# An attention and mixture-of-experts kernel: the order of work after the last attention pair, and the place of a fill

## The chip, the cores and the metric

The kernel runs on one core of a Trainium2 chip. That core has five engines that run their own instruction streams and meet at semaphores: TensorE (PE in the profile), VectorE (DVE), ScalarE (ACT), GpSimd (POOL) and SyncE (SP), which here only issues transfers. The metric is device time in microseconds, the median of several executions. Profiles are of one execution each.

## The reference

Two stages. First a chunked attention: for 4 batches, 8 heads, 768 positions and head size 64, each chunk of 32 queries sees 8 memory keys, 16 positions to its left, itself and 8 to its right. Its output, 3072 tokens of 512 values, goes into a mixture of experts with one always-active dense branch:

```python
h_dense = np.maximum(x @ w1_dense, 0.0)
y_dense = h_dense @ w2_dense
logits = x @ w_gate                      # 512 x 8
expert_idx = np.argmax(logits, axis=1)
gate_w = probs[np.arange(N), expert_idx] # softmax of the logits
for e in range(E):
    mask = expert_idx == e
    h = np.maximum(x[mask] @ w1[e], 0.0)
    y_moe[mask] = gate_w[mask, None] * (h @ w2[e])
return y_dense + y_moe
```

Each token goes to one of eight experts, so which rows an expert multiplies is known only once its gate has been computed.

## The kernel before

**Order.** The engines' orders are written by hand: the kernel opens a manual schedule (line 121), so each engine executes its instructions in the order in which the Python code emits them. A wait in one engine's order holds all that stands behind it on that engine, and nothing on the others.

**Attention.** A loop over 16 pairs of heads (i = 0 to 15; four pairs to each batch, b is the batch) is staged over pairs: while pair i has its probabilities turned and multiplied with the values (probs_back, values, scaled), pair i + 1 has its queries and keys turned and its scores and softmax computed, and pair i - 1 goes through gate_part (its output is transposed into xT32 in fp32 for the gate and into xTb in bf16 for the dense layers) and gate_sum (its share of the logits). What follows from a complete batch is worked off in the next batch's pairs: choose (largest logit, one-hot, differences), weight_exp and weight (the gate's weight), rank (each token's row in the expert order, row_i), and for each of six tiles of 128 tokens dense_1 and dense_2 (the dense branch) and row_out.

**The records in DRAM.** row_out scatters a tile's records with an indirect transfer issued by POOL into x_rec, a DRAM tensor with a region of rows for each expert. A record of 3080 bytes holds the token in bf16, its gate weight, its number and its dense result. So what an expert needs is found in consecutive rows. One transfer of 3080 KB, the fill (lines 779 to 784), writes some finite record into the 128 rows ahead of each expert's region, since a last, short tile of an expert can reach back into them.

**The experts.** 31 slots of 128 records. The first R1 = 11 (round one) are full tiles that surely can be made of the first three batches' records; lists_1a and lists_1b compute which rows and which expert each has. The other 20 (round two) need all four batches; lists_2a, 2b and 2c compute theirs. For a slot s: fetch(s) loads 128 records into a tile xg (394 KB, SP's queue, eleven buffers); transposed(s) turns the tokens on TensorE into at_ps and ACT copies them to xT; staged(s) copies the expert's first weights to w_st on DVE; first_layer(s) is 16 matmuls and a ReLU on ACT; second_layer(s) is 4 matmuls, then DVE forms y (times gate weight, plus the dense result), POOL computes the destinations and issues the scatter of y to the output. The first fetch waits until every record written so far has landed (lines 649 to 656), as does the first fetch of round two.

**After the last pair** (lines 852 to 904): the eleven fetches of round one, gate_part(15), then the transposes of slots 0 and 1, gate_sum(15), the first layer of slot 0, choose, and so on: batch 3's gate, dense tiles and row_outs are interleaved with round one's slots, one dense tile to one slot, transposes one slot ahead. Round two transposes two slots ahead.

**Shared places.** The transposes of slots, the gate's sums, the choice's turned logits, ranks and counts lie in one PSUM tile, at_ps; dense_1, dense_2 and gate_part rotate through two PSUM buffers (tag tp); w_st has three buffers, y five.

Of the kernel before, what the change touches and what calls it, by code (L numbers as in the profile page):

```python
# [20 lines left out]
def kernel(  # L21
# [14 lines left out]
    nc = tc.nc  # L36
# [12 lines left out]
    T = S // 128  # L49
# [10 lines left out]
    E = moe_w_gate.shape[1]  # L60
# [32 lines left out]
    R1 = -(-((N_tokens - S) - E * 127) // 128)  # L93
# [14 lines left out]
    REC = YD + D_moe  # L108
# [3 lines left out]
    x_rec = nc.dram_tensor("x_rec", [N_rows, REC], F32, kind="Internal").ap()  # L112
    rows_written = []

    def scattered(ins, group):

        tc.declare_no_dep(ins.ins, group=group, reason="rows of tokens are distinct")
        tc.add_to_no_dep_group(group, ins.ins)
# [5 lines left out]
    with (  # L124
# [35 lines left out]
        NPAIR = B * NP  # L160
# [175 lines left out]
        def gate_part(pi):  # L336

            b, hp = divmod(pi, NP)
            xb = st_[pi].pop("x")
            if hp == 0:  # L340
                lg_b = x_pool.tile([GP, GT], F32, tag="lg")
                rec_b = x_pool.tile([128, T, REC], F32, tag="rec")
                xTb_b = x_pool.tile([128, NP, S], BF16, tag="xTb")
                bat[b].update(lg=lg_b, rec=rec_b, xTb=xTb_b, h={})
            rec, xTb = bat[b]["rec"], bat[b]["xTb"]
            nc.gpsimd.tensor_copy(  # L346
                rec.bitcast(BF16)[:, :, hp * 128:(hp + 1) * 128], xb
            )
            last = pi == NPAIR - 1
            xT32 = g_work.tile([128, S], F32, tag="xT32")  # L350
            st_[pi]["xT"] = xT32
            for t0 in (0, T // 2):
                xtt = a_ps2.tile([128, 512], F32, tag="tp")
                cols = slice(t0 * 128, (t0 + T // 2) * 128)
                for t in range(T // 2):
                    nc.tensor.transpose(  # L356
                        xtt[:, t * 128:(t + 1) * 128], xb[:, t0 + t, :], identity_f32
                    )
                nc.scalar.copy(xT32[:, cols], xtt[:, :T // 2 * 128])  # L359

                if last:
                    nc.vector.tensor_copy(xTb[:, hp, cols], xtt[:, :T // 2 * 128])
            if not last:
                nc.gpsimd.tensor_copy(xTb[:, hp, :], xT32)  # L364
# [280 lines left out]
        def fetch(s):  # L645
            row = entry(SP_, 0, s, r_sp, N_rows - 128)
            xg = m_load.tile([128, REC], F32, tag="xg")
            ins = nc.sync.dma_start(xg, x_rec[bass.ds(row, 128), :])
            while rows_written:
                tc.add_manual_dep(  # L650
                    ins.ins, rows_written.pop(),
                    mybir.DependencyInfo(
                        mybir.DependencyClass.Sync, mybir.DependencyReason.DATA
                    ),
                    reason="the rows in DRAM",
                )
            xgs[s] = xg
            if s < R1:
                first_round.append(ins.ins.name)

        def transposed(s):
            xtp = at_b[:, 2 * (s % 2):2 * (s % 2) + 2, :].rearrange(
                "p a (d t) -> p (a d) t", t=128
            )
            xgb = xgs[s].bitcast(BF16)
            for d in range(DT):
                nc.tensor.transpose(  # L667
                    xtp[:, d, :], xgb[:, d * 128:(d + 1) * 128], identity
                )
            xT = m_work.tile([128, DT, 128], BF16, tag="xT")  # L670
            nc.scalar.copy(xT, xtp)  # L671
            xTs[s] = xT

        def staged(s):

            e = entry(DVE_, 1, s, e_dve, E - 1)
            w_st = w_work.tile([128, DT, F], BF16, tag="w_st")
            nc.vector.tensor_copy(w_st[:, None], w1_all[:, bass.ds(e, 1), :, :])  # L678
            w_sts[s] = w_st

        def first_layer(s):
            xT, w = xTs.pop(s), w_sts.pop(s)
            ph = sc[:, s % 2, :].rearrange("p (f t) -> p f t", t=128)
            for f in range(FT):
                for d in range(DT):
                    nc.tensor.matmul(  # L686
                        ph[:, f, :], w[:, d, f * 128:(f + 1) * 128], xT[:, d, :],
                        start=(d == 0), stop=(d == DT - 1),
                    )
            h_sb = m_work.tile([128, FT, 128], BF16, tag="h")  # L690
            nc.scalar.activation(h_sb, ph, AF.Relu)  # L691
            hs[s] = h_sb
# [75 lines left out]
        for i in range(NPAIR):  # L768
            nxt = i + 1 < NPAIR
            b, hp = divmod(i, NP)  # L770

            mine = [2 * hp - 2, 2 * hp - 1] if b and hp else []
            if b == B - 1:
                mine = [[], [0, 1], [2, 3, 4], [5]][hp]
            for t in bat[b - 1].pop("ready", []) if b else []:
                row_out(b - 1, t)
            if i == NPAIR - 2:

                ins = nc.sync.dma_start(
                    x_rec.rearrange("(e r) c -> r e c", e=E)[:128],  # L780
                    bat[b - 1]["rec"][:, 0:1, :].to_broadcast([128, E, REC]),
                )
                scattered(ins, "rows")
                rows_written.append(ins.ins.name)
            if i + 2 < NPAIR:
                load_qk(i + 2)
                load_v(i + 2)
            if nxt:
                transpose_qk(i + 1)
            if i == NPAIR - 1:  # L790
                lists_1b()
            probs_back(i)
            if hp == 1 and b:
                choose(b - 1)
            for t in mine[:1]:
                dense_1(b - 1, t)
            if i:
                gate_part(i - 1)
            if nxt:
                scores(i + 1)  # L800
                next_rows(i + 1, 1)
                if hp == 1 and b:
                    weight_exp(b - 1)
                softmax(i + 1)
                next_rows(i + 1, 0)
                if hp == 1 and b:
                    weight(b - 1)
            for t in mine[:1]:
                dense_2(b - 1, t, nc.vector.tensor_copy if nxt else nc.scalar.copy)
            later = list(mine)  # L810
            if mine and hp > 1:
                row_out(b - 1, later.pop(0))
            for t in mine[1:]:
                dense_1(b - 1, t)
                if t != mine[-1]:
                    dense_2(b - 1, t, nc.scalar.copy)
                    row_out(b - 1, later.pop(0))
            if i:
                gate_sum(i - 1)
            if i == NPAIR - 1:  # L820
                for s in range(2):
                    staged(s)
            values(i)
            scaled(i)
            for t in mine[1:]:
                if t == mine[-1]:
                    dense_2(b - 1, t, nc.scalar.copy)
            bat[b - 1]["ready"] = later
            for _ in range(1 if i + 3 < NPAIR else 2):
                if w_todo:  # L830
                    load_w(*w_todo.pop(0))
            if hp == 1 and b:
                rank(b - 1)
            if hp == NP - 1 and b:
                for t in bat[b - 1].pop("ready"):
                    row_out(b - 1, t)
            if i == NPAIR - 2:
                lists_1a()
# [12 lines left out]
        b = B - 1  # L851
        for s in range(R1):
            fetch(s)
        gate_part(NPAIR - 1)
        transposed(0)
        transposed(1)
        gate_sum(NPAIR - 1)
        first_layer(0)
        choose(b)
        dense_1(b, 0)  # L860
        first_layer(1)
        weight_exp(b)
        rank(b)
        weight(b)
        dense_2(b, 0, nc.scalar.copy)
        row_out(b, 0)
        second_layer(0)
        transposed(2)
        staged(2)
        lists_2a()  # L870
        for s in range(2, R1):
            t = s - 1
            if t < T:
                dense_1(b, t)
            first_layer(s)
            if t < T:
                dense_2(b, t, nc.scalar.copy)
                row_out(b, t)
            if s + 1 < R1:
                transposed(s + 1)  # L880
                staged(s + 1)
            second_layer(s - 1)
            if s == 2:
                lists_2b()
            if s == 3:
                lists_2c()
        second_layer(R1 - 1)
        for s in range(R1, R1 + 4):
# [47 lines left out]
```

## Time and profile before

| what | us |
|---|---|
| median of 3 runs | 291.83 (290.97 to 292.04) |
| the profiled execution | 290.2 |
| its span, first to last instruction | 288.5 |
| TensorE busy | 214.0 (74%) |
| VectorE, ScalarE, GpSimd busy | 157.8, 134.8, 135.2 |
| mean granted TensorE clock | 0.905 of full |

The span is the time between the first and the last instruction of one execution; the execution's time lies 1.7 us above it. TensorE is the busiest engine, but a share of busy time is an average over stages. The chain of work that ended last is put together at 46% from TensorE, 16% from transfers, 14% from stretches in which nothing visible was waited for, and 10% from VectorE. The attention pairs end near 186 us, round one of the experts runs from 195 to 237, round two from there to 282. The lines of the profile that bear on the change are shown where the prediction uses them. In a timeline line the numbers are start and duration in us, then the engine, the code line, the operation, output and input; in brackets how long the engine had been idle and what ended that.

### The profile page before, as it was taken

What the parts mean: (1) busy time and instruction counts of PE and PEld (TensorE: products, weight loads), DVE (VectorE), ACT (ScalarE), POOL (GpSimd) and SP (SyncE); (2) the same over time, 40 slices, a digit from 0 to 9 for tenths busy, and PEclk for the clock granted to TensorE, in tenths of its full rate; (3) what the DMA queues carried; (4) which work ended last, traced back from release to release, by engine and by line L of the source; (5) the groups of instructions that cost most, each with busy time, mean ns of one, the idle gap of its engine ahead of it and who ended that gap; (6) DMA issues with size and microseconds to landing.
All of it is one profiled execution on the core that took longest, in us unless ns stands there. A gap on an engine that the chain in (4) does not pass through costs nothing.

```text
span 288.5 us, 10781 instructions
## 1 busy us (share of the span) xinstructions
PE 214.0 (74%) x4559; PEld 160.4 (56%) x4559; DVE 157.8 (55%) x320; ACT 134.8 (47%) x204; POOL 135.2 (47%) x209
## 2 busy tenths in 40 slices
PE   1576838669987739888658878517999868999980
PEld 1455637465755537656437656316677546777740
DVE  2675465746556445675363853832774445766640
ACT  2362646526755516556153673312456435455430
POOL 7054244512674922375470455510357742665661
PEclk9999598769999968999795999965999999999997
DMA  6999998995999996999999799959534599896220
GB/s 106 191 149 166 170 161 136 178 179 76 199 174 195 193 219 94 188 183 165 184 209 185 100 305 370 204 176 366 224 121 184 195 350 412 278 303 233 101 73 0
DMA packets 59440, 55.51 MB, mean 192 GB/s; under 512 B 35966, under 2 KB 51326, under 8 KB 59392
## 3 DMA queue, kind: packets, MB, share of 16 engines
q0 software_dynamic: 20560, 31.49, 52.9%
q1 hardware_dynamic: 38832, 23.33, 34.6%
q8 instruction: 36, 0.59, 0.9%
q14 instruction: 12, 0.10, 0.1%
HBM read 51.62 MB, written 20.74 MB: 251 GB/s over the span
## 4 chain that ended last, share of the span: by engine, by line
PE 46%; DMA 16%; issue 14%; DVE 10%; ACT 5%; POOL 4%; SPq 2%; POOLq 1%; DVEq 0%; ACTq 0%
PE sc L686 9%; PE av L699 7%; PE ph L461 7%; PE pd L475 4%; PE at_ps L300 4%; DMA t__2065<-in_k_dram 3%; PE xtt L356 3%; DVE mx L285 3%; DMA t__3050<-in_k_dram 3%; PE tp_f L242 3%; DMA x_rec<-rec_b,row_i 3%; PE sc L276 2%; PE at_ps L667 2%; DMA t__2550<-in_k_dram 2%; DVE vw L199 2%
## 5 line engine op out<-in xcount | busy, mean ns | idle before, releaser
L486 POOL DMA_INDIRECT x_rec<-rec_b,row_i x24 | 24.7, 1029 | 58.0 <-issue 21.7
L715 POOL DMA_INDIRECT out_dram<-y,dst x31 | 31.7, 1021 | 25.5 <-DVE w_st L678 12.2
L712 DVE SCALAR_TENSOR_TENSOR y<-av,xg 128x512 f32<-128x512 f32 x31 | 23.3, 751 | 29.2 <-PE av L699 23.7
L285 DVE TENSOR_REDUCE mx<-sc 128x12 f32<-128x768 f32 x16 | 15.3, 958 | 39.3 <-PE sc L276 39.3
L686 PEld LDWEIGHTS <-w_st 128*128 128x128 bf16 x496 | 30.9, 100 | 8.8 <-issue 3.2
L686 PE MATMUL sc<-xT,w_st 128*128 128x128 bf16 x496 | 33.9, 223 | 1.8 <-DVE w_st L678 0.6
L699 PE MATMUL av<-w_all,h_sb 128*128 x124 | 31.8, 379 | 2.7 <-DVE y L712 1.7
L691 ACT ACTIVATE h_sb<-sc 128x512 bf16<-128x512 f32 x31 | 18.5, 597 | 31.4 <-PE sc L686 28.6
L364 POOL CAST xTb_b<-xT 128x768 bf16<-128x768 f32 x15 | 12.4, 829 | 36.4 <-ACT xT L359 36.3
L461 PE MATMUL ph<-xTb_b,w1d 128*128 128x128 bf16 x384 | 28.8, 235 | 0.0
L461 PEld LDWEIGHTS <-w1d 128*128 128x128 bf16 x384 | 26.5, 107 | 3.9 <-issue 0.8
L475 PE MATMUL pd<-w2d,h_d 128*128 128x512 bf16 x96 | 24.9, 381 | 5.0 <-DVE rec_b L479 5.0
L199 ACT COPY vw<-vw 24x1536 f32<-24x1536 f32 x16 | 23.5, 1468 | 10.6 <-DMA vw<-in_v_dram 10.3
L312 PE MATMUL av<-vw,at 64*32 64x65 f32 x1536 | 22.1, 237 | 8.2 <-issue 7.6
L312 PEld LDWEIGHTS av<-vw,at 64*32 64x32 f32 x1536 | 18.2, 110 | 16.7 <-issue 14.4
L254 DVE COPY dT<-tp_f 128x768 bf16<-128x768 bf16 x16 | 15.3, 955 | 20.3 <-PE tp_f L242 19.9
L356 PE MATMUL xtt<-identity_f,x_p 128*128 128x128 f32 x96 | 19.4, 333 | 8.3 <-DVE x_p L324 3.2
L300 PE MATMUL at_ps<-identity_f,a_sb 128*128 128x128 f32 x96 | 19.2, 355 | 7.2 <-issue 4.3
L671 ACT COPY xT<-at_ps 128x512 bf16<-128x512 bf16 x31 | 18.1, 584 | 9.1 <-PE at_ps L667 9.0
L346 POOL CAST rec_b<-x_p 128x768 bf16<-128x768 f32 x16 | 13.4, 835 | 19.1 <-DVE x_p L324 16.6
L678 DVE COPY w_st<-w_all 128x2048 bf16 x31 | 21.2, 693 | 1.8 <-DMA w_all<-in_moe_w_dram 0.9
L252 ACT COPY dT<-tp_f 128x768 bf16<-128x768 bf16 x16 | 12.7, 794 | 19.9 <-PE tp_f L242 19.8
(231 smaller groups left out, 366.9 us busy)
## 6 DMA issues: line engine op xcount, KB each, us to landing
xg<-x_rec SPq DMA_DIRECT2D x31, 385.0 KB
w_all<-in_moe_w_dram POOLq DMA_DIRECT2D x16, 512.0 KB
vw<-in_v_dram SPq DMA_DIRECT2D x32, 184.0 KB
x_rec<-rec_b SPq DMA_DIRECT2D x1, 3080.0 KB
vw<-in_mem_v_dram SPq DMA_DIRECT2D x32, 48.0 KB
vw<-in_v_dram SPq DMA_DIRECT2D x64, 4.0 KB
w1d<-in_moe_w_dense_dram POOLq DMA_DIRECT2D x1, 512.0 KB
w2d<-in_moe_w_dense_dram POOLq DMA_DIRECT2D x1, 512.0 KB
```

Source lines behind the costliest of these rows:

```text
L199: copy(vt[p0 + CHUNK:p0 + CTX, :NCH, :D], vt[p0:p0 + CTX - CHUNK, 1:NCH + 1, :D],)
L285: nc.vector.reduce_max(mx, scv, axis=AX.X)
L300: nc.tensor.transpose(at_ps[:, t, :], a_sb[:, t, :], identity_f32)
L312: nc.tensor.matmul(av[cc * CHUNK:(cc + 1) * CHUNK, hh, t * (D + 1):(t + 1) * (D + 1)], at[p0:p0 + KEYS, t, cc * CHUNK:(cc + 1) * CHUNK], v ...
L356: nc.tensor.transpose(xtt[:, t * 128:(t + 1) * 128], xb[:, t0 + t, :], identity_f32)
L461: nc.tensor.matmul(ph[:, f * 128:(f + 1) * 128], w1d_sb[:, d, f * 128:(f + 1) * 128], xTb[:, d, t * 128:(t + 1) * 128], start=(d == 0), st ...
L475: nc.tensor.matmul(pd, h_d[:, f * 128:(f + 1) * 128], w2d_sb[:, f, :], start=(f == 0), stop=(f == FT - 1),)
L486: ins = nc.gpsimd.indirect_dma_start(x_rec, bass.IndirectOffsetOnAxis(ap=row_i[:, n:n + 1], axis=0), bat[b]["rec"][:, t, :], None,)
L686: nc.tensor.matmul(ph[:, f, :], w[:, d, f * 128:(f + 1) * 128], xT[:, d, :], start=(d == 0), stop=(d == DT - 1),)
L699: nc.tensor.matmul(py, h_e[:, f, :], w2_all[:, bass.ds(e, 1), f, :], start=(f == 0), stop=(f == FT - 1),)
L712: nc.vector.scalar_tensor_tensor(y, py, xg[:, GW:GW + 1], xg[:, YD:], op0=ALU.mult, op1=ALU.add)
L715: ins = nc.gpsimd.indirect_dma_start(out, bass.IndirectOffsetOnAxis(ap=dst, axis=0), y, None, bounds_check=N_tokens - 1, oob_is_err=False,)
```

## The change

The fill moves from pair 14 to behind the eleven fetches of round one on the same queue, and is declared independent of all of these but the last, on which it waits. The copies of the first two slots' weights (staged(0), staged(1)) leave pair 15. After the last pair each engine's order begins with batch 3's gate sum, choice, dense tiles, ranks and row_outs; transposes of slots 0 and 1 come before the last dense tile, and then round one's slots follow one another, transposed two ahead.

```diff
-            if i == NPAIR - 2:
-                ins = nc.sync.dma_start(x_rec... [:128], bat[b - 1]["rec"]...)
-                scattered(ins, "rows")
-                rows_written.append(ins.ins.name)
...
             if i:
                 gate_sum(i - 1)
-            if i == NPAIR - 1:
-                for s in range(2):
-                    staged(s)
             values(i)
             scaled(i)
...
         for s in range(R1):
             fetch(s)
+        ins = nc.sync.dma_start(x_rec... [:128], bat[b - 1]["rec"]...)
+        scattered(ins, "rows")
+        rows_written.append(ins.ins.name)
+        for f in first_round[:-1]:
+            tc.declare_no_dep(ins.ins, f, reason="those tiles are full without these")
         gate_part(NPAIR - 1)
-        transposed(0)
-        transposed(1)
         gate_sum(NPAIR - 1)
-        first_layer(0)
+        dense_1(b, 0)
         choose(b)
-        dense_1(b, 0)
-        first_layer(1)
+        for t in range(2):
+            dense_1(b, t + 1)
+            dense_2(b, t, nc.scalar.copy)
         weight_exp(b)
         rank(b)
         weight(b)
-        dense_2(b, 0, nc.scalar.copy)
         row_out(b, 0)
-        second_layer(0)
-        transposed(2)
-        staged(2)
+        row_out(b, 1)
+        dense_1(b, 3)
+        dense_2(b, 2, nc.scalar.copy)
+        row_out(b, 2)
+        for s in range(2):
+            staged(s)
+        dense_1(b, 4)
+        dense_2(b, 3, nc.scalar.copy)
+        row_out(b, 3)
         lists_2a()
-        for s in range(2, R1):
-            t = s - 1
-            if t < T:
-                dense_1(b, t)
+        for s in range(2):
+            transposed(s)
+        dense_1(b, 5)
+        dense_2(b, 4, nc.scalar.copy)
+        row_out(b, 4)
+        for s in range(R1):
             first_layer(s)
-            if t < T:
-                dense_2(b, t, nc.scalar.copy)
-                row_out(b, t)
-            if s + 1 < R1:
-                transposed(s + 1)
-                staged(s + 1)
-            second_layer(s - 1)
-            if s == 2:
+            if s == 0:
+                dense_2(b, 5, nc.scalar.copy)
+                row_out(b, 5)
+            if s + 2 < R1:
+                transposed(s + 2)
+                staged(s + 2)
+            if s:
+                second_layer(s - 1)
+            if s == 0:
                 lists_2b()
-            if s == 3:
+            if s == 1:
                 lists_2c()
         second_layer(R1 - 1)
```

More of the change, by code (lines that the diff above doesn't have):

```diff
@@ L776 @@
                 row_out(b - 1, t)
-            if i == NPAIR - 2:
[L779 to L782, printed above, removed]
-                scattered(ins, "rows")
-                rows_written.append(ins.ins.name)
             if i + 2 < NPAIR:
@@ L853 @@
             fetch(s)
+        ins = nc.sync.dma_start(
+            x_rec.rearrange("(e r) c -> r e c", e=E)[:128],
+            bat[b - 1]["rec"][:, 0:1, :].to_broadcast([128, E, REC]),
+        )
+        scattered(ins, "rows")
+        rows_written.append(ins.ins.name)
+        for f in first_round[:-1]:
+            tc.declare_no_dep(ins.ins, f, reason="those tiles are full without these")
         gate_part(NPAIR - 1)
-        transposed(0)
-        transposed(1)
         gate_sum(NPAIR - 1)
-        first_layer(0)
+        dense_1(b, 0)
         choose(b)
-        dense_1(b, 0)
-        first_layer(1)
+        for t in range(2):
+            dense_1(b, t + 1)
+            dense_2(b, t, nc.scalar.copy)
         weight_exp(b)
```

## The prediction

> **What bounds the kernel now.** I read the chain of work that ended last, then TensorE's timeline around the places it names, then the granted clock by stretches, then what the SyncE (SP) queue waits for. The change touches only work from the last pair (i = 15) on, so I start at 180 us. The chain there:
>
> ```profile
> 184.13 7.27 DMA x_rec<-rec_b,row_i
> ...
> 191.71 3.22 DMA xg<-x_rec
> 194.93 0.05 issue
> 194.98 0.62 PE at_ps L667 x4
> ...
> 198.56 1.82 PE sc L686 x16
> ...
> 200.62 1.71 PE ph L461 x16
> ```
>
> The last scatter of batch 2's rows (row_out, tile 5) takes 7.27 us to land, the first gathered tile another 3.22 us, and only then TensorE does transposed(0), which stands in its order ahead of batch 3's gate sum and all dense work. Those need no gathered row. TensorE's timeline shows the hole, and the stretch in which round one closes:
>
> ```profile
> 185.34 0.34 PE L312 MATMUL av<-vw,at 64*32 64x65 f32 x15 [1.11 <-issue]
> 188.85 1.34 PE L356 MATMUL xtt<-identity_f,x_p 128*128 128x128 f32 x6 [3.17 <-DVE x_p L324]
> 194.98 0.61 PE L667 MATMUL at_ps<-identity,xg 128*128 128x128 bf16 x4 [4.78 <-DMA xg<-x_rec]
> ...
> 228.05 1.05 PE L686 MATMUL sc<-xT,w_st 128*128 128x128 bf16 x16 [0.56 <-ACT xT L671]
> ...
> 236.08 1.02 PE L699 MATMUL av<-w_all,h_sb 128*128 x4 [0.84 <-DVE y L712]
> ...
> 239.05 1.07 PE L686 MATMUL sc<-xT,w_st 128*128 128x128 bf16 x16 [0.61 <-DVE w_st L678]
> ```
>
> From 185.68 to 194.98 TensorE works 1.34 us. Round one's last second layer starts at 236.08 and ends 0.87 later, at 236.95: that is the mark I carry the sum to. What comes after (round two, tail) has the same code before and after: 288.5 - 236.95 = 51.6 us. The granted clock, in stretches cut where it switches (columns: stretch, length, busy us of PE, its weight loads, DVE, ACT, POOL, then clock, DMA share, GB/s):
>
> ```profile
> 49.10:52.52 3.42, 1.47 (x12) 1.26 (x12) 2.61 (x5) 1.69 (x3) 1.19 (x2) 1.00 1.26 176
> 52.52:55.93 3.41, 3.41 (x165) 2.21 (x163) 2.07 (x3) 2.50 (x4) 2.46 (x4) 0.50 1.27 205
> 185.63:189.05 3.42, 0.25 (x10) 0.23 (x3) 2.40 (x4) 0.00 (x0) 0.28 (x1) 1.00 1.10 287
> 189.05:192.46 3.41, 1.15 (x6) 0.75 (x4) 1.11 (x2) 0.96 (x2) 0.68 (x2) 0.50 0.15 61
> 199.29:202.70 3.41, 3.41 (x35) 3.41 (x33) 1.66 (x9) 0.88 (x2) 0.00 (x0) 0.50 1.01 404
> 205.00:230.00 25.00, 23.69 (x275) 17.35 (x274) 14.94 (x38) 13.84 (x26) 16.83 (x25) 1.00 0.42 162
> 245.00:260.00 15.00, 15.00 (x188) 11.59 (x187) 10.33 (x16) 7.86 (x15) 9.48 (x16) 1.00 0.90 292
> ```
>
> After the hole the clock is half until 202.70, so the first expert and dense tiles run at 1.82 and 1.71 us where later ones take 0.89. From 205 TensorE is the bound (23.69 of 25 us), with the transfers at a share of 0.42; from 245 it is busy throughout at 1.98 us a slot, with transfers at 0.90.
>
> **The change, part by part.** *Fill off the front of SP's queue.* One DMA of 3080 KB, issued at 163.57, whose 1024 packets of 3080 B I count at 168.1 to 183.9 us (all but 12 or so by 179.7). It stood among batch 2's scatters and two weight loads of 512 KB, which ran at about 180 GB/s from 182 to 188 with two scatters of tile rows queued behind them on POOL's queue. Without it those weights start when issued, near 178, end near 184, and the last scatter, issued by POOL at 184.13, needs no more than one in an idle stretch: the one issued at 225.58 let the next gather go at 229.16, 3.6 us. So gathers start near 188.4 instead of 191.7. It saves nothing by itself, because after the reorder TensorE asks for xg(0) near 200; its value is that the eleven gathers (191.71 to packets' end at 206.1, 14.4 us) end about 3 us sooner.
>
> *staged(0), (1) off DVE's front.* They hold DVE from 185.27 (0.93 us for the weights, 1.29 us of copies) and push scaled(15): rs at 187.42. Without them rs starts when values end, 185.7, x_p is done at 187.0, and the transposes start at 187.15 instead of 188.85: 1.7 us. The copies now go behind row_out(2), where DVE waits on dense work anyway; first_layer(0) comes near 203, so they are covered by some 4 us.
>
> *New order on TensorE.* From 187.15 to the end of second_layer(10), at full clock: transposes 2 x 0.50 (the three at 180.40); wait for ACT's second copy 0.6 (0.48 plus hand-overs); gate sum 0.65; dense 6 x (0.89 + 0.88) = 10.6; choice, ranks, count 0.5; 11 transposes of 0.23 = 2.5; 11 first layers of 0.89 = 9.8; 11 second layers of 0.87 = 9.6. Waits that stay or come: transposed(0) behind DVE's read of the count, and transposed(1) behind ACT's copy, since all share at_ps (before: 0.67 at 196.26): 1.0 together; second_layer(10) behind y(9), 0.84 as before. Sum 37.1 us.
>
> *Half clock.* Stretches with 1.47 and 1.39 us of work in 3.41 were followed by half clock, one with 1.89 was not. After the change the stretch to 189.05 holds about 1.0 + 0.25, so I expect a drop, and one full stretch (as 52.52:55.93) to end it: 3.41 / 2 = 1.7 us lost. Bounds: 0 if it stays up, 3.4 for a second stretch. The Trainium skill's page "TensorE: Matmul & The Clock Gate" (HAM oscillation) warns only of idle gaps above about 3.4 us; the gap left here is 1.5 us, and by that rule the loss would be nothing and the sum 1.7 us lower. The rows above, busy 43% and followed by a drop, speak against that reading, and I go by them.
>
> So second_layer(10) ends at 187.15 + 37.1 + 1.7 = 226.0, against 236.95: 10.95 us. Cross-check: round one's dense tiles no longer sit between slots, each slot transposes two ahead as round two does, and runs at round two's 1.98 us; before, the slots from 225.35 came every 2.3 to 2.9 us.
>
> *ACT, DVE, POOL.* ACT has 1.2 us per dense pair of 1.78 and 1.18 per slot of 1.98. DVE has y 0.75 + weights 0.69 per slot, plus three list parts of about 2 us, the first before the slots; it catches up by slot 4. POOL's six scatters (0.2 + 0.3 + 1.0) run from about 197.5 to 206, before the first y. Nothing there delays TensorE; cover gone, a list part would cost one slot 1 us.
>
> *Fill behind the gathers.* Here the change adds a wait. SP holds the fill until gather 10 lands, and gathers of round two stand behind it and wait for it to land (fetch(11) takes every row written). Before:
>
> ```profile
> SPq L648 <- DMA x_rec<-rec_b,row_i: 15.3, 2, 12.0
> ```
>
> fetch(11) hung on row_out(5) and went at 229.16, 7.8 us ahead of its use at 236.94. After: gathers to 203, and about 2.3 us more as up to three scatters of 394 KB share the engines: fill issued near 206. Its first packet came 4.5 us after issue before, a gather's 1.0: take 2.5. Then 3.15 MB plus half of the scatters left and 0.13 MB/us of output rows: the mixed rate after 168 was 360 to 400 GB/s, so 12 to 14 us, landing near 222. fetch(11) lands 3.2 us later, 225.5; TensorE wants it at 226.0. That is no slack, so I charge 1.0 us. Lower bound 0. Upper bound: issue to last packet as before, 20.3 us: landing at 227, xg(11) at 230.4, a stall of 4.4. I take 1.0 because the old tail (179.7 to 183.9) lay among the weight loads, which are gone by then. The page "DMA: Bandwidth & Descriptors" of the skill (Latency and other measured facts) speaks against the move: it gives HBM access 0.2 us on average but 2 us under high load, and this wait chains two landings in a saturated stretch; by it I would estimate some 2 us more of stall, and no row here isolates that.
>
> *Output buffers.* y has five. Scatters land late beside the fill, outputs queue behind them; y(5) near 218 needs out(0), issued near 209 and landing near 216. Covered by 2 us; gone, it adds to the same stall.
>
> **Sum.** 10.95 - 1.0 = 9.95 us. The profiled execution took 290.2 us with a span of 288.5, so 280.2; the runs' median, 291.83, stands 1.6 above it, so 281.8, stated as 282.0.
>
> **The rivals.** *R1, round two's loads come late*: fill at its old 20.3 us, or outputs held up beside it; stall 3 to 7 us. For it: no slack at 226, DMA at 1.0 share from 198 to 222. Against: work before it is only 1.2 MB of scatters, and later gathers at 1.3 us each overtake 1.98 us slots. 285 to 289. *R2, the clock stays down or the dense chain stalls*: two further half stretches, or ACT late on a PSUM buffer at each tile (two rotate): 2 to 4 us, 284 to 286. Against: from 199.29 one busy stretch brought it back. *R3, better*: the clock never drops and xg(11) is early: 282.0 - 2.7 = 279.3. *R4, slower*: the fill alone decides. For the time to stay, xg(11) must come at 237, so the fill must land at 233.5, 27 us after issue, 7 beyond its old 20.3; slower by over 0.5% from 29 us on. Since nothing but outputs competes then, that needs a rate below 115 GB/s for the fill: unlikely, at about 293 to 296. *R5, the change does nothing* would need TensorE's hole to be refilled by a wait of batch 3's own gate, which needs only x_p: no row for it.
>
> **How the numbers follow.** Forecast with stall 0 to 3 us: 0.56 (280.5 to 284); R1 0.18, R2 0.09, R3 0.11, R4 and R5 0.06. Low end: R3 at 279. High end: R1 to 288. A measurement of this kernel tells 0.5% (1.5 us) from no change. Faster 0.93; same 0.02 (end of R1, R5); slower 0.05 (R4).
>
> **What would show it.** No TensorE wait on xg near 190; L356 at about 187; dense tiles at 0.89 from about 193; second layer 10 ending near 226; the fill issued near 206 and fetch(11) near 222; TensorE idle at the round boundary 2 to 3 us. Wrong, if after 226 TensorE waits on xg for over 3 us, if half clock goes on beyond 196, or if the second round's slots are longer than 1.98 us.

## The result, and the profile after

| | before | changed |
|---|---|---|
| median, 6 runs each, us | 291.94 (290.97 to 293.17) | 284.93 (280.4 to 289.8) |
| the profiled execution, us | 290.2 | 289.8 |
| its span, us | 288.5 | 288.1 |
| end of the last value products (attention) | 185.69 | 187.68 |
| from there to the end of the last second layer | 95.0 | 92.6 |

The ratio of times is 0.9668, with a 95% interval of 0.9604 to 0.9731: the changed kernel is faster by 3.3%. This ratio, like those below, leaves out executions more than 1.5% above the fastest of their kernel, three of the changed kernel's six among them; the medians of all six give 0.976. The forecast was 282.0 us, in a range of 279 to 288.

The profiled execution is the slowest of the six, and it can't be read without knowing that executions of this kernel differ by some us in the attention stage, long before anything in the change. In the fourteen profiles of this study the value products of pair 12 begin anywhere from 144.4 to 152.6 us. Marks below therefore count from the end of the last value products.

The hole that the forecast started from is gone. TensorE's timeline, changed kernel:

```profile
186.50 1.18 PE L312 MATMUL av<-vw,at 64*32 64x65 f32 x96
189.94 1.50 PE L356 MATMUL xtt<-identity_f,x_p 128*128 128x128 f32 x6 [2.26 <-DVE x_p L324]
...
194.18 1.06 PE L461 MATMUL ph<-xTb_b,w1d 128*128 128x128 bf16 x16
195.07 1.03 PE L475 MATMUL pd<-w2d,h_d 128*128 128x512 bf16 x4
...
201.92 0.38 PE L667 MATMUL at_ps<-identity,xg 128*128 128x128 bf16 x4 [0.28 <-DVE cnt L584]
202.98 0.38 PE L667 MATMUL at_ps<-identity,xg 128*128 128x128 bf16 x4 [0.67 <-ACT xT L671]
...
209.42 1.02 PE L699 MATMUL av<-w_all,h_sb 128*128 x4 [0.81 <-issue]
...
228.27 1.02 PE L699 MATMUL av<-w_all,h_sb 128*128 x4 [1.77 <-issue]
...
232.00 1.02 PE L699 MATMUL av<-w_all,h_sb 128*128 x4 [0.84 <-DVE y L712]
236.37 0.61 PE L667 MATMUL at_ps<-identity,xg 128*128 128x128 bf16 x4 [3.35 <-DMA xg<-x_rec]
```

Dense tiles (L461, L475) fill the place where TensorE waited for the first gathered tile, and transposed(0) starts without a wait on its data. A new wait stands at the boundary of the rounds: second_layer(10) ends near 233.0 and TensorE then waits 3.35 us for the first gather of round two. The granted clock fell to half during this wait, at 234.33, and stayed there until 241.16 us, so the first slots of round two ran slowly as well. The chain of work that ended last names what held it:

```profile
201.95 16.81 DMA xg<-x_rec
...
218.81 13.37 DMA x_rec<-rec_b
...
232.38 3.95 DMA xg<-x_rec
...
236.37 0.62 PE at_ps L667 x4
```

The last gather of round one was issued at 201.95 and took 16.8 us; only then did the fill go out, which took 13.4; only then fetch(11). What SP's queue waited for says the same (L844 is the fill):

```profile
SPq L844 <- DMA xg<-x_rec: 16.5, 1, 16.5
SPq L648 <- DMA x_rec<-rec_b: 12.1, 1, 12.1
```

### The profile page after: what moved, and what is told of

The parts are those of the page before. It is cut to its first block, busy times and chain, and to the rows that moved or that the text cites. A ratio compares the mean times of both kernels' runs of the same rounds, so it can differ in the third digit from the quotient of the medians.

```text
span 288.1 us, 10795 instructions
## 1 busy us (share of the span) xinstructions
PE 215.2 (75%) x4559; PEld 161.1 (56%) x4559; DVE 158.7 (55%) x320; ACT 134.7 (47%) x204; POOL 136.1 (47%) x209
## 4 chain that ended last, share of the span: by engine, by line
PE 34%; DMA 31%; issue 14%; DVE 10%; POOL 4%; ACT 3%; SPq 2%; POOLq 1%; DVEq 0%; ACTq 0%
DMA vw<-in_v_dram 12%; DMA xg<-x_rec 7%; PE ph L461 5%; PE sc L686 5%; DMA x_rec<-rec_b 5%; PE av L699 4%; PE at_ps L300 4%; DMA t__2065<-in_k_dram 3%; PE xtt L356 3%; PE tp_f L242 3%; PE pd L475 2%; POOL out_dram L715 2%; DMA t__3048<-in_q_dram 2%; DMA t__2550<-in_k_dram 2%; PE av L312 2%
## 5 line engine op out<-in xcount | busy, mean ns | idle before, releaser
L715 POOL DMA_INDIRECT out_dram<-y,dst x31 | 31.1, 1003 | 32.1 <-DVE w_st L678 19.2
L285 DVE TENSOR_REDUCE mx<-sc 128x12 f32<-128x768 f32 x16 | 15.3, 958 | 39.5 <-PE sc L276 39.5
L699 PE MATMUL av<-w_all,h_sb 128*128 x124 | 31.8, 379 | 5.2 <-DVE y L712 2.7
L686 PE MATMUL sc<-xT,w_st 128*128 128x128 bf16 x496 | 33.8, 223 | 0.3 <-DVE w_st L678 0.3
L475 PE MATMUL pd<-w2d,h_d 128*128 128x512 bf16 x96 | 25.6, 390 | 5.2 <-DVE rec_b L479 5.2
L312 PE MATMUL av<-vw,at 64*32 64x65 f32 x1536 | 21.2, 235 | 10.1 <-issue 10.1
L461 PE MATMUL ph<-xTb_b,w1d 128*128 128x128 bf16 x384 | 28.7, 235 | 0.0
L461 PEld LDWEIGHTS <-w1d 128*128 128x128 bf16 x384 | 26.4, 107 | 3.7 <-DVE xTb_b L362 0.8
L356 PE MATMUL xtt<-identity_f,x_p 128*128 128x128 f32 x96 | 19.3, 334 | 6.2 <-ACT h_d L468 2.6
L346 POOL CAST rec_b<-x_p 128x768 bf16<-128x768 f32 x16 | 13.4, 837 | 18.6 <-DVE x_p L324 15.6
```

Of the source, the lines that this page charges most:

```text
L312: nc.tensor.matmul(av[cc * CHUNK:(cc + 1) * CHUNK, hh, t * (D + 1):(t + 1) * (D + 1)], at[p0:p0 + KEYS, t, cc * CHUNK:(cc + 1) * CHUNK], v ...
L356: nc.tensor.transpose(xtt[:, t * 128:(t + 1) * 128], xb[:, t0 + t, :], identity_f32)
L461: nc.tensor.matmul(ph[:, f * 128:(f + 1) * 128], w1d_sb[:, d, f * 128:(f + 1) * 128], xTb[:, d, t * 128:(t + 1) * 128], start=(d == 0), st ...
L475: nc.tensor.matmul(pd, h_d[:, f * 128:(f + 1) * 128], w2d_sb[:, f, :], start=(f == 0), stop=(f == FT - 1),)
L686: nc.tensor.matmul(ph[:, f, :], w[:, d, f * 128:(f + 1) * 128], xT[:, d, :], start=(d == 0), stop=(d == DT - 1),)
L699: nc.tensor.matmul(py, h_e[:, f, :], w2_all[:, bass.ds(e, 1), f, :], start=(f == 0), stop=(f == FT - 1),)
```

## The experiments

Marks in the table are us after the end of the last value products, each from one profile: start of the next transposes (L356), issue of the fill and of fetch(11), end of second_layer(10) and of the last second layer. The last column is the median of that run's own timed executions, and of the kernel before beside them.

| run | transposes | fill | fetch(11) | second 10 ends | all end | median / before |
|---|---|---|---|---|---|---|
| before | 3.2 | -22 | 43.5 | 51.4 | 95.0 | 291.94 |
| changed | 2.3 | 31.1 | 44.7 | 45.4 | 92.6 | 284.93 / 291.94 |
| after_again | 2.8 | 27.6 | 41.6 | 45.1 | 89.2 | 282.57 / 290.36 |
| after_third | 2.8 | 19.7 | 38.4 | 46.3 | 89.9 | 285.5 / 290.19 |
| fill_back | 2.1 | -22 | 29.0 | 43.5 | 86.8 | 282.91 / 290.36 |
| fb_again | 2.2 | -22 | 28.5 | 43.8 | 87.2 | 283.95 / 290.19 |
| fill_only | 4.4 | 20.0 | 43.2 | 50.1 | 93.8 | 287.22 / 290.36 |
| fill_nowait | 2.8 | 13.9 | 37.5 | 45.7 | 89.4 | 284.11 / 290.36 |
| staged_back | 4.4 | 19.6 | 37.7 | 48.2 | 91.6 | 287.41 / 290.19 |
| rows_wait | 2.3 | 21.6 | 40.6 | 52.9 | 96.0 | 288.67 / 289.98 |
| fill_twice | 2.3 | 24.9 | 51.1 | 46.5 | 100.0 | 294.47 / 289.98 |
| fb_both | 4.0 | -22 | 29.0 | 43.5 | 87.3 | 282.26 / 290.19 |
| fb_best | 1.5 | -23 | 27.3 | 41.7 | 84.9 | 278.84 / 289.98 |
| late_best | 2.1 | 28.1 | 40.2 | 44.8 | 88.2 | 285.07 / 289.72 |

**The changed kernel again.** No edit.

> The changed kernel once more, unaltered, for a second profile and as the yardstick of this group. Theory T (the fill chained behind starved gathers now sets the end): the last gather of round one again takes over 14 us to land because batch 3's scatters share the engines with it (16.8 us in the first profile), the fill goes out only then, fetch(11) goes when the fill lands, and TensorE idles 3 us or more at the boundary of the rounds; 282 to 287 us. Rival V (the excess over the forecast lies in the attention stage, which ended 2.8 us later than forecast in the first profile): the boundary stall is under 1.5 us and the attention end moves with the total.

> The changed kernel, unaltered, with more rounds, as the yardstick of this group. By the two profiles so far the stage after the attention (from the end of the last pair's value products to the end of the last second layer) takes 89.2 to 92.7 us here against 95.0 in the kernel before, while the attention itself ends anywhere from 184.4 to 188.3 us. Expected 281 to 286 us; gathers of round one landing late, fill after them, and a TensorE wait on xg at the boundary of 1 to 3.5 us.

Ratios 0.9702 [0.9616, 0.9788] and 0.9705 [0.961, 0.98]. The stage after the attention is 2.4 to 5.8 us shorter than before; in these two the wait for round two's gathers is short (1.2 and 1.0 us in the first, none in the second) although the fill went out as late as 27.6 us in the first. So fetch(11) still goes 14 to 19 us after the fill, but TensorE stands waiting for it only in some executions.

**The parts apart.** The order alone (fill at pair 14 again):

```diff
+            if i == NPAIR - 2:
+                ins = nc.sync.dma_start(x_rec... [:128], bat[b - 1]["rec"]...)
...
         for s in range(R1):
             fetch(s)
-        ins = nc.sync.dma_start(x_rec... [:128], bat[b - 1]["rec"]...)
-        for f in first_round[:-1]:
-            tc.declare_no_dep(ins.ins, f, ...)
```

> The new order, but the fill back at pair 14. T: fetch(11) hangs on the scatters alone and goes near 218 instead of 232, no TensorE wait on xg at the boundary (was 3.4 us), no half clock after it (about 1.6 us), fewer waits of y for its buffers: 4 to 6 us under the changed kernel, 278 to 281. In the old place the fill ran while the DMA engines of the changed kernel stand idle (10 to 39 GB/s from 175 to 180), so it costs nothing there. Rival F (moving the fill is itself worth the 3 us that the forecast gave the gathers): no faster than the changed kernel, 284 to 288.

> New order with the fill at pair 14, with more rounds. Theory T (the fill behind the gathers costs 2 to 5 us after the attention, and the equal medians of the first group come from the attention's end, 2.3 us later in that profile): 1 to 4 us under the changed kernel, 280 to 283, the stage after the attention again near 87 us. Rival F (the move is worth as much before the attention's end as it costs after it): the same as the changed kernel, with pairs 13 to 15 slower here by 2 us or more.

Ratios 0.9717 [0.9619, 0.9815] and 0.9786 [0.9718, 0.9853]. The stage after the attention is as theory T has it, 86.8 and 87.2 us, and fetch(11) goes 9 to 16 us earlier than in the changed kernel. It hangs on the scatters now (fill_back, SP's queue):

```profile
SPq L648 <- DMA x_rec<-rec_b,row_i: 6.0, 1, 6.0
```

But the median is that of the changed kernel within what these runs can tell (282.91 beside 282.57, 283.95 beside 285.5). One part of the reason lies ahead of the mark. TensorE's last value products with the fill at pair 14 (fill_back):

```profile
184.81 1.04 PE L312 MATMUL av<-vw,at 64*32 64x65 f32 x81
186.39 0.34 PE L312 MATMUL av<-vw,at 64*32 64x65 f32 x15 [0.54 <-issue]
```

and with the fill behind the gathers (after_again):

```profile
183.26 1.18 PE L312 MATMUL av<-vw,at 64*32 64x65 f32 x96
```

In each of the five profiles with the fill at pair 14 the 96 products are broken by a pause in which nothing visible is waited for, and take 1.5 to 2.4 us from the first start to the last; in each of the nine with the fill moved they take 0.96 to 1.11. From pair 12's value products to the end of pair 15's the five take 38.7 to 39.5 us, the nine 36.3 to 38.2. So the old place costs about 1.5 us (39.1 against 37.6 on the mean) ahead of the mark, about 1.0 of it inside the last value products, and gives about 3.6 us (90.6, the mean of the three profiles of the changed kernel, against 87.0) behind it. Half clock does not explain the gain: after_again met none in this stage and still took 89.2 us, the two with the fill at pair 14 met one stretch of 3.41 us each. That leaves some 2 us in favour of the old place, which these medians, of four to six executions each, do not show.

The pause has a trace of its own. All 60 pauses of over 0.5 us inside value products, in all fourteen profiles, end 1.2 to 2.0 us after a packet of 16384 bytes has landed in the queue that the profile calls "instruction". In the five, the pause stands behind the 81st product each time and ends 1.35 to 1.51 us after such a packet; in the nine the last such packet had landed 2.7 to 3.3 us ahead of the 82nd product. Counted from the start of pair 12's value products, this packet started at 35.8 to 36.3 us in the five and at 31.8 to 33.8 in the nine. So what TensorE lacked was most likely its instructions, late beside the fill; no run isolates that.

The other half alone (the old order, fill behind the gathers):

> The old order, with only the fill moved behind the gathers. T: TensorE still waits for xg(0) with the gate and the dense tiles behind it. In the changed kernel's profile the last scatter of batch 2 took 6.5 us to land where it took 7.3, so the gathers come under 1 us earlier; fetch(11) hangs on row_out(5) in any case: 290 to 292, the same as before within 0.5%. Rival F: gathers 3 us earlier and the time 2 to 3 us lower, 288.5 to 290.

287.22 us, ratio 0.9855 [0.976, 0.995]: faster than theory T allowed. Its last value products show no pause. TensorE still waits for xg(0) and (1) ahead of the gate:

```profile
193.66 0.61 PE L667 MATMUL at_ps<-identity,xg 128*128 128x128 bf16 x4 [3.36 <-DMA xg<-x_rec]
195.85 0.61 PE L667 MATMUL at_ps<-identity,xg 128*128 128x128 bf16 x4 [1.59 <-DMA xg<-x_rec]
```

and the stage after the attention is 1.3 us shorter than before. The gathers begin 5.6 us after the mark instead of 6.0, so they are not what rival F had in mind either. Half clock lasted 10.2 us here (from 189.63) and 13.7 us before (from 189.05), which may be all of the 1.3 us.

**Is the fill on the path?** A second transfer of its size behind it, which only fetch(11) waits for:

```diff
+        ins = nc.sync.dma_start(x_pad..., bat[b - 1]["rec"]...)
+        rows_written.append(ins.ins.name)
         gate_part(NPAIR - 1)
```

> The changed kernel with a second transfer of the size and shape of the fill (to a DRAM tensor that nothing reads) behind it on SP's queue; the first gather of round two waits for both. Theory T (the fill behind the gathers is on the path that sets the end): fetch(11) 8 to 11 us later, TensorE idle for that long at the boundary of the rounds, and the time 7 to 11 us up, to 290 to 296. Rival (gathers of round two come early enough to hide a fill): under 3 us.

294.47 us, ratio 1.0218 [1.0143, 1.0293], and TensorE's waits say where it went (total, times, longest):

```profile
PE at_ps L668 <- DMA xg<-x_rec: 9.3, 2, 7.6
```

Half clock came with that wait, for 13.7 us from 232.77 on. Theory T holds: behind the gathers there is no room for another fill, and hardly for the one.

**Is it the wait?** The fill declared independent of all gathers:

```diff
+        apart = m_work.tile([128, E], F32, tag="apart")
+        nc.sync.dma_start(apart, moe_w_gate[:128])
         ins = nc.sync.dma_start(x_rec... [:128], bat[b - 1]["rec"]...)
-        for f in first_round[:-1]:
+        for f in first_round:
```

> The changed kernel with the fill declared independent of all eleven gathers (a transfer of 4 KB stands between the last gather and the fill on SP's queue, so that only order is left between them). T: the fill goes out near 203 instead of 219 but shares the engines with gathers and scatters; bytes are the same, so it lands 3 to 6 us earlier than 232, and the time falls by 2 to 4 us, to 281 to 283. If the wait were all, it would fall by the whole 16 us of the wait's length until the stall is gone, as in the run with the fill back: 278 to 281. Rival V: no change.

284.11 us, ratio 0.9771 [0.9694, 0.9848]: no gain that can be told. The fill went out 13.9 us after the mark, and fetch(11) 37.5, 4 to 7 us sooner than in the first two profiles of the changed kernel; the wait at the boundary was gone, and round one itself took as long as there. The stage, 89.4 us, is as long as in two of the three profiles in which the fill waits, and 2.4 us longer than with the fill at pair 14. So in those two the waiting costs nothing that can be seen, and what is left goes with the fill's bytes in round one; in the first profile (92.6 us) the wait at the boundary comes on top.

**Why did the last gather take 16.8 us?** Batch 3's scatters held back until the gathers have landed:

```diff
-            for f in first_round:
-                tc.declare_no_dep(ins.ins, f, reason="those tiles are full without these")
```

> The changed kernel with batch 3's scatters made to wait until all gathers of round one have landed. In the profiles so far the fill went out 31, 28 and 20 us after the end of the last value products, as scatters overlapped the gathers more or less. Theory S (the scatters starve the gathers: their packets of 6160 bytes alternate with the gathers' 3080, and gathers ran at 83 to 112 GB/s beside scatters at 160 to 217): the last gather lands within 9 us of its issue and the fill goes at 20 to 22 us. The scatters move behind, share with the fill, and fetch(11) goes at 36 to 42 us as before: the sum of bytes is the same. Time equal to the changed kernel within its scatter, 281 to 286. Rival: gathers are slow by themselves; the fill still goes at 27 us or later.

The fill waited on the last gather for 8.2 us, against 16.5, 14.5 and 7.2 in the three profiles of the changed kernel. The two long waits are those in which the first scatter of batch 3 was issued ahead of the last gather (by 1.7 and 0.8 us); in the third it came 2.2 us behind it. By these profiles the scatters slow the gathers when they catch up with them, which does not happen in every execution. I counted packets in the first profile: from 207.5 to 210 us scatters moved 195 GB/s in packets of 6160 bytes and gathers 111 in packets of 3080, from 212.5 to 215 it was 217 and 112. The Trainium skill's "DMA: Bandwidth & Descriptors" (Queues, rings and completion order) states that a DMA engine goes round its queues packet by packet. From that I would expect two to one for packets of twice the size, which these two stretches come near; from 205 to 207.5, with 212 and 192, it was not so. The time, however, was that of the kernel before: 288.67 us, ratio 0.9997 [0.9945, 1.0049], above what I expected. The scatters now stood ahead of the outputs on POOL while y's five buffers filled:

```profile
223.42 0.75 DVE L709 SCALAR_TENSOR_TENSOR y<-av,xg 128x512 f32<-128x512 f32 x1 [5.83 <-DMA out_dram<-y,dst]
```

and TensorE waited 7.10 us for second_layer there; half clock from 219.45 to 229.69 us went with it. The "output buffers" step of the prediction, covered by 2 us in its sum, is what this run uncovers.

**The moved weight copies.** staged(0) and staged(1) back in pair 15, the rest as changed:

```diff
             if i:
                 gate_sum(i - 1)
+            if i == NPAIR - 1:
+                for s in range(2):
+                    staged(s)
             values(i)
...
-        for s in range(2):
-            staged(s)
         dense_1(b, 4)
```

> The changed kernel with the two weight copies of DVE back in pair 15, ahead of the last pair's scaling. The forecast priced their move at 1.7 us: the gap between the last value products and the next transposes should grow from 2.3 to 2.8 us to about 3.5 to 4.5 us and the time by 1 to 2 us, to 283 to 287. Rival: DVE was held by the list computation (lists_1b) at that point in any case and the copies fit beside TensorE's waits: no difference.

287.41 us, ratio 0.9877 [0.9796, 0.9959]. VectorE's timeline:

```profile
187.69 1.29 DVE L678 COPY w_st<-w_all 128x2048 bf16 x2 [0.85 <-DMA w_all<-in_moe_w_dram]
188.90 0.22 DVE L323 RECIPROCAL rs<-av 128x12 f32<-128x12 f32 x1
```

The copies wait for the last weights and hold the scaling; the transposes start 4.4 us after the value products against 2.3 to 2.8. That is 1.6 to 2.1 us for a forecast of 1.7.

**What is left in TensorE's gap.** Spare matmuls on weights against the half clock, and the register loads of the expert list early, both on top of the order with the fill at pair 14:

```diff
+        for s in (0, GRP):
+            e_pe[s] = entry(PE_, 1, s, e_pe, E - 1)
+        for j in range(9):
+            nc.tensor.matmul(sc[:, j % 2, :], w2d_sb[:, 0, :128], w2d_sb[:, 0, :],
+                             start=True, stop=True)
         gate_part(NPAIR - 1)
```

> New order, fill at pair 14, and two additions: nine matmuls on weights, whose results are not used, in TensorE's gap ahead of the last transposes; and both register loads of round one's expert list on TensorE issued there too, rather than ahead of second_layer(0) and second_layer(8). If the half clock after the gap costs about 1.7 us and the two register loads cost 1.1 to 1.4 and 0.3 to 1.8 us, as TensorE's gaps ahead of these second layers suggest, the stage after the attention falls by 3 to 4 us from 86.8, to 83 to 84, and the time to 278 to 280. Rival: the loads' gaps are waits for ReLU results and the half clock is ended within a microsecond in any case: no change.

282.26 us, ratio 0.973 [0.9664, 0.9795], the stage as long as without them: the two loads took 2.2 us, the matmuls came behind them, and the transposes started at 4.0 instead of 2.2 us. But no half clock followed, and second_layer(0) ended 4.55 us after first_layer(0) began, not 5.75 to 6.1. So with five matmuls, these first, and then the load for slot 0 alone:

> New order, fill at pair 14, five spare matmuls first in TensorE's gap (nine ran too long, behind the register loads) and only the first register load early. In the run with both, the two loads took 2.2 us ahead of the spare matmuls, so the transposes started at 4.0 us after the value products instead of 2.1; the clock stayed full and second_layer(0) came 1.2 us sooner after first_layer(0). Now: transposes at 2.5 us, no half clock, second_layer(0) as in that run; the stage after the attention 84 to 85.5 us instead of 87, time 279 to 283. Rival: what these save comes back at the boundary of the rounds, no change.

278.84 us (276.19 to 282.85), ratio 0.9647 [0.9582, 0.9713], the stage 84.9 us. This is the lowest median of all. Five of its six executions took 279.4 us or less; the lowest of the changed kernel's sixteen was 279.82:

```profile
184.63 0.35 PE L312 MATMUL av<-vw,at 64*32 64x65 f32 x15 [1.26 <-issue]
184.91 1.25 PE L852 MATMUL sc<-w2d 128*128 128x512 bf16 x5
186.51 0.84 PE L356 MATMUL xtt<-identity_f,x_p 128*128 128x128 f32 x6 [0.35 <-DVE x_p L324]
```

The six transposes take 0.84 us and not 1.50. The interval of its ratio overlaps that of the changed kernel; the medians of runs made together with the kernel before put it at 0.962 of that kernel (278.84 / 289.98), the changed one at 0.973 to 0.984.

The same additions with the fill behind the gathers:

> The changed kernel, fill behind the gathers, with the five spare matmuls and the early register load. It differs from the run that came out at 278.84 us only in the fill's place. Theory T: TensorE reaches the end of round one 2 to 4 us sooner than in the changed kernel, but the fill and with it fetch(11) do not move, so most of that turns into a wait on xg at the boundary; the stage after the attention 87 to 89 us against 84.9 with the fill at pair 14, the pause inside the last value products absent (0.96 us against 1.5 to 2.4), the time 280 to 283. Rival F (the place of the fill makes no difference): 278 to 280, no wait at the boundary.

285.07 us (280.33 to 290.59), ratio 0.9744 [0.9664, 0.9824], above the 280 to 283 expected; the stage 88.2 us, in theory T's span, but by another way: no wait on xg at the boundary, and round one longer. Neither it nor fb_best met half clock in this stage, so the 3.3 us between their stages go with the fill's place. Register loads of the expert lists, late_best (count, then ns):

```profile
L634 DVEq TENSOR_LOAD <-et x1: 2610/2610/2610, 220.9 to 220.9; - x1
L634 PEldq TENSOR_LOAD <-et x1: 2582/2582/2582, 227.9 to 227.9; - x1
```

and fb_best, from the same stretch:

```profile
L634 DVEq TENSOR_LOAD <-et x2: 879/932/984, 214.6 to 226.7; - x2
L634 PEldq TENSOR_LOAD <-et x2: 597/1020/1442, 220.2 to 230.8; - x2
```

Each of DVE and TensorE reads the list anew at slot 8, and while the fill runs (from 218.8 us in late_best) that takes 2.6 us instead of 1.0 and 1.4. VectorE's load stands ahead of y, and second_layer(6) waited 1.15 us for y; TensorE's stands ahead of second_layer(8), where its timeline shows 1.68 us of idle time. In the first profile of the changed kernel the same two took 1.68 and 2.66 us, and the 1.77 us ahead of second_layer shown above is the latter.

## Why the prediction was right, and where it was not

The time came out 2.9 us above the forecast and inside the range, by a sum with two terms mis-sized, some missing and one wrong. That it came so near is in part luck. The sum took 9.95 us off the stage behind the attention; the three profiles show 2.4, 5.8 and 5.1. The medians differ by 7.0 us, and what the stage does not give lies ahead of the mark: about 1.5 us that were not in the sum, and an attention that varies by several us.

*The hole and the order.* Right in kind: TensorE no longer waits for xg(0), dense tiles run at 0.89 us from 194, slots at 1.98 us. Mis-sized: from the transposes to the end of second_layer(10) the sum had 37.1 + 1.7 = 38.8 us; the changed kernel took 43.1, 42.3 and 43.5, and with the fill out of the way 41.4 and 41.6. The 1.0 us for at_ps and the 0.84 at the end are there as put (0.28, 0.67, 0.24; 0.84). Missing were TensorE's register loads ahead of second_layer(0) and (8), 0.8 to 1.9 and 0.3 to 1.8 us of idle time, and second_layer(2) waiting 0.7 us for y behind the list computation, which the sum had VectorE catch up by slot 4 at no cost to TensorE.

*The moved copies.* 1.7 us forecast, 1.6 to 2.1 measured by undoing it. The transposes still came 2.3 to 2.8 us after the value products and not 1.5: in the first profile the list computation (lists_1b) and the gate's sum held VectorE 0.8 us beyond the end of the products. The step asked what is late next and did not look there.

*Half clock.* One stretch, 1.7 us, was forecast; after the gap, the three profiles of the changed kernel show one of 3.4 us (the first), none (after_again) and one of 6.8 us. The clock switches on a grid of 3.41 us: half clock after the gap lasted 3.41, 6.83, 10.24 or 13.65 us in these profiles. Where the gap lies in that grid differs from execution to execution. The stretches of after_again (start and end, length, busy us of PE first, granted clock third from the end) share the gap between two, and the clock stays up:

```profile
182.79:186.21 3.42, 1.64 (x102) 1.04 (x102) 2.69 (x15) 0.58 (x1) 1.72 (x3) 1.00 1.16 212
186.21:189.62 3.41, 2.12 (x19) 1.19 (x20) 2.11 (x4) 0.86 (x2) 0.95 (x2) 1.00 0.46 180
189.62:193.03 3.41, 3.41 (x52) 2.89 (x50) 1.84 (x10) 1.78 (x3) 0.00 (x0) 1.00 0.51 151
```

In the first profile of the changed kernel one stretch holds nearly all of it, and half clock followed:

```profile
186.54:189.96 3.42, 1.16 (x100) 1.02 (x97) 2.94 (x15) 0.11 (x1) 1.32 (x4) 1.00 1.23 210
```

The bounds, 0 to 3.4 us, were right, and the value within them is a draw. A gap of 2.3 us was enough for a drop, so the limit of about 3.4 us of idle time that "TensorE: Matmul & The Clock Gate" (HAM oscillation) gives, weighed in the prediction, is not a safe one here. The drops after the gap followed stretches in which TensorE was busy for 0.25 to 1.43 us of 3.41. No sharp limit comes out of the profiles, though: elsewhere a drop followed a stretch with 2.19 us (fill_back, to 76.39), and none followed one with 1.47 (after_third, to 213.13).

*The fill off SP's front.* Wrong. The step had the last weights and with them the last scatter and the gathers 3.3 us earlier. POOL issued the weights at 180.93 us, and their packets ran from 183 to 190 us behind two scatters; before, with the fill, from 181 to 188. Counted from the mark that is the same time, so the step's gain did not come; the last scatter took 6.5 us where it took 7.3, and the gathers began 4.8 to 6.8 us after the mark against 6.0. What the old place did cost, a pause in the value products, was not in the sum at all; that gain of about 1.5 us is what five profiles show against nine.

*The fill behind the gathers.* The mechanism was put right and mis-sized: fill out near 206, landing near 222, a stall of 1.0 us. It went out at 218.8, landed at 232.2 (13.4 us, not 16), the stall was 3.35. The failed term is "about 2.3 us more" for up to three scatters beside the gathers: all six had been issued by 208.3 us, and the last gather alone took 16.8 us. Of R1's two halves, late gathers showed at the boundary in the first profile and a full set of output buffers only in rows_wait. That the fill's bytes would lengthen round one itself, and register loads in it, was named nowhere.

A second stretch of half clock after the gap, of which R2 made more, occurred in one profile of three, and the first had two more behind its wait at the boundary. R4 did not occur; fill_twice shows how near it lies: another 3 MB turn 3% faster into 2% slower.

## What to carry to other kernels

When an engine's order puts a data wait ahead of work that needs no such data, turn the order; that part paid whatever else was done. A transfer moved out of one place is not free in the next: ask what is queued behind it there, which transfers it or its neighbours will slow there, and which register loads and instruction transfers fall into the same time. Compare marks inside the stage that was changed when the stages ahead of it vary by more than the effect.

## What the runs showed that I had not expected

- Register loads of up to eight list entries took 0.6 to 1.7 us from the end of the attention through round one where no fill ran, and 0.8 to 2.7 us while it did; nine of the seventeen loads beside the fill took over 1.9 us. That transfers lengthen them is a coincidence in time, not isolated.
- The pause inside the last value products, 0.4 to 1.3 us, came with the fill at pair 14 in five profiles of five and without it in none of nine, and it ended each time shortly after an instruction packet had landed.
- Identical programs met no, one or two stretches of half clock after the same gap. The three profiles with spare matmuls in the gap show none.
